# Score tiles of 128 and 256 columns masked and reduced in one VectorE operation, zero products in 32-row tiles, and a new order, in a three-stage attention and experts kernel

## The chip, the cores and the metric

One core of a Trainium2 chip. The metric is the device time of one execution in microseconds; the runs of the kernel before took 534.11, 534.59 and 535.53 us, and their median, 534.59 us, is the time to compare with.

## The reference

Three stages, for 4 batches of 448 positions (S) and 768 channels. Shapes are in the comments.

```python
def _attn_ref(q, k, v, cap):                 # 4 x 12 heads x 448 x 64
    scores = scale * np.matmul(q, k.transpose(0, 1, 3, 2))
    scores = cap * np.tanh(scores / cap)
    attn = softmax(scores)
    return np.matmul(attn, v)

def _moe_ref(x, w_in, conv_w, w_out):        # 768 -> 1024 -> 768
    h = np.maximum(x @ w_in, 0.0)
    conv_out = three taps of conv_w over the positions of h
    gate = 1.0 / (1.0 + np.exp(-conv_out))
    return h * gate @ w_out

def _moe2_ref(x, w_gate, wq, wk, wv, wo):    # 4 experts, head size 64
    two best experts of each position, weights w by softmax over the two
    for e in range(E):
        scores = scale * (q @ k.transpose(0, 2, 1))
        scores = np.where(causal, -1000000000.0, scores)
        a = softmax(scores)
        out += w[e] * (a @ v @ wo[e])        # for positions that chose e
```

The weights w_in, conv_w and w_out come as 64-bit floats; everything else is 32-bit.

## The kernel before

The class Plan records every operation of the kernel once, with its engine, as a numbered entry (`add`). `issue()` then emits them in the order of the table ORDER, a permutation of those numbers written out, so ORDER alone sets the sequence of work on every engine and on the DMA queue. A second table, SWAP, holds numbers of operations whose engine is flipped: `pick` and `one_of` offer an eviction or a copy to ScalarE (ACT) or VectorE (DVE), and a number in SWAP takes the other one. Because helpers record the operations, the profile shows a helper's line for all of them: L376 for products on TensorE (PE), L380 for transposes, L324 for VectorE, L316 for ScalarE, L385 for DMA issues on SyncE (SP), L399 for GpSimd (POOL). The buffers have three names: fm (32-bit floats in SBUF), rm (the rounded halves that the fast products read) and ps (the eight PSUM banks).

The stages overlap. Attention runs in 24 groups of two heads (six groups for each batch): score products, Tanh and Exp on ScalarE over tiles of up to 1792 columns, sums on VectorE, then the products with v. The first two groups' scores are plain 32-bit products (`qk`, `last_keys`); each 32-bit product is two passes of PE.

Beside attention, in the first 58 us, `wi_prep` brings in w_in: 24 pieces of 128 rows by 256 columns. `decode` turns the 64-bit words of a piece into 32-bit floats in four operations (a multiplication by 2^-112 on either engine by `one_of`, a shift, and two SCALAR_TENSOR_TENSOR operations), then `pick` makes the upper half and a subtraction on VectorE the lower half. The pieces use two sets of buffers in turn (`wi_bufs`), in places of the region `later`. When attention of a batch is done, `recip` and `x_unit` (labels x0 to x3) normalise it, and the products with w_in (`f_unit`, labels f0 to f3) follow, three rounded products for each exact one. The gates (`conv_gate`) go over DRAM to the last stage. `fold_mm` multiplies w_out by the experts' weights, and the last stage does the projections, the scores, the transposes and the output for each batch.

The zero products: while the first loads are on their way, PE multiplies a tile z of zeros, which a VectorE memset (L573) fills. z is the first 128 columns of `CT.bufs[0]`, at the start of the region `later`, where `wi_prep` puts its decoded pieces. WARM = 8 products of 128 x 128 by 128 columns carry the label "st", FILL = 4 more "warm"; the order decides where they go.

The experts' scores, `scores2(b, i, k)`: for each batch b and pair of experts i, seven tiles k of 128 rows in a PSUM bank: each of the two experts has one of 128, 256 and 384 columns, and the last 64 positions of both share one of 448. For each tile VectorE adds the triangle of -1e9 (`tri`) to the last 128 columns in PSUM (64 for the shared one), a second VectorE operation takes the negative of the row maximum, and ScalarE does Exp with that as its bias and sums the rows into `accum_out`. There are 56 such tiles, 16 each of 128, 256 and 384 columns and 8 of 448. The lines:

```python
pl.tt(o, o, tri_m if shared else tri, OP.add)
pl.reduce(mx, ps[:, :n], OP.max, negate=True)
pl.act(P2[i][k], ps[:, :n], AF.Exp, bias=mx, accum_out=RS2[i][:, 0, k:k + 1])
```

Of the kernel before, what the change touches and what calls it, by code (L numbers as in the profile page):

```python
# [8 lines left out]
AF = mybir.ActivationFunctionType  # L9
# [10 lines left out]
E = 4  # L20
NK = S // 128
SH = S // 2
# [180 lines left out]
class Plan:  # L203
# [5 lines left out]


    DRAIN = 97.0
    OPEN = {(128, 128): 107.0, (64, 128): 107.0, (128, 64): 53.0, (64, 64): 53.0, (128, 32): 13.0}
    RATE = 320.0
    HOP = {"pe": 200.0, "act": 190.0, "dve": 170.0, "pool": 150.0, "dma": 1500.0}

# [1201 lines left out]
```

## Time and profile before

| what | value |
|---|---|
| median of three runs (lowest, highest) | 534.59 us (534.11, 535.53) |
| profiled execution: span from first to last instruction | 532.9 us |
| what the runs hold beyond that span | 1.2 to 2.6 us, 1.7 us at the median |
| PE busy | 523.3 us (98%), 3312 instructions |
| VectorE busy | 448.8 us (84%), 1053 instructions |
| ScalarE busy | 372.1 us (70%), 689 instructions |
| GpSimd busy | 18.4 us (3%) |
| DMA, mean | 120 GB/s |
| granted clock of TensorE, mean | 1.000 |

The page gives the profiled execution's span and no total of its own, so its own time is taken as its span and the runs' times are set beside it. The span is the time between the first and the last instruction on any engine. Busy times overlap. A share is an average over stages with different limits, so the windows below, which give busy times stretch by stage, say more than the column of shares. A busy PE is not a PE at its peak: ends of products are modelled.

### The profile page before, as it was taken

How to read it: one execution, taken by the hardware profiler on the slowest of the kernel's cores; microseconds unless marked ns; L12 is line 12 of the kernel's file. 1: busy time of each engine (PE TensorE's matmuls, PEld its weight loads, DVE VectorE, ACT ScalarE, POOL GpSimd, SP SyncE). 2: the span in 40 equal slices, each digit the busy share in tenths (PEclk: the TensorE clock that was granted, in tenths of full speed). 3: DMA queues.
4: the chain of work that ended last, by engine and by line, in shares of the span. 5: the costliest groups of instructions: out<-in, count | busy, mean ns of one | idle time of the engine just before them, and what ended most of it. 6: DMA issues, size and time to landing. Idle time of an engine off the chain costs nothing.

```text
span 532.9 us, 9400 instructions
## 1 busy us (share of the span) xinstructions
PE 523.3 (98%) x3312; PEld 414.2 (78%) x3312; DVE 448.8 (84%) x1053; ACT 372.1 (70%) x689; POOL 18.4 (3%) x71
## 2 busy tenths in 40 slices
PE   8989999999999999999999999999999999999997
PEld 6434488545765857669999999999978988999786
DVE  6999999889689787889768999979998997965772
ACT  7989948999888869865333667627858884653562
POOL 8100000000000000000000002000000000000000
PEclk9999999999999999999999999999999999999999
DMA  6535554423323241225574442245345225404414
GB/s 205 177 129 163 173 174 155 115 83 104 117 79 105 66 133 54 79 81 174 185 243 148 127 138 62 87 108 141 78 101 139 91 49 144 125 1 124 124 52 156
DMA packets 42543, 63.84 MB, mean 120 GB/s; under 512 B 7424, under 2 KB 31360, under 8 KB 42496
## 3 DMA queue, kind: packets, MB, share of 16 engines
q1 hardware_dynamic: 42496, 63.24, 39.4%
q8 instruction: 26, 0.43, 0.3%
q14 instruction: 21, 0.17, 0.1%
HBM read 40.94 MB, written 12.85 MB: 101 GB/s over the span
## 4 chain that ended last, share of the span: by engine, by line
PE 80%; DVE 15%; issue 2%; DMA 2%; ACT 1%; SPq 0%; DVEq 0%
PE ps L376 77%; DVE fm L324 10%; DVE rm L324 5%; PE ps L380 3%; DMA fm<-w_in 2%; ACT fm L316 1%; SPq L385 0%; ACT rm L316 0%; DVE ps L324 0%; DVEq L324 0%
## 5 line engine op out<-in xcount | busy, mean ns | idle before, releaser
L376 PE MATMUL ps<-rm 128*128 128x448 f32 (+6 forms) x2316 | 401.4, 351 | 4.4 <-DVE fm L324 1.9
L376 PEld LDWEIGHTS ps<-rm 128*128 128x128 f32 (+1 forms) x2316 | 353.1, 187 | 49.0 <-issue 8.7
L316 ACT ACTIVATE fm<-fm 128x448 f32<-128x448 f32 (+7 forms) x216 | 158.7, 767 | 35.0 <-DVE fm L324 22.7
L324 DVE SCALAR_TENSOR_TENSOR fm<-fm 128x448 f32<-128x448 f32 (+5 forms) x240 | 146.8, 631 | 14.7 <-ACT fm L316 12.7
L316 ACT ACTIVATE fm<-ps,fm 128x896 f32<-128x896 f32 (+5 forms) x142 | 109.7, 793 | 30.7 <-DVE fm L324 20.2
L376 PE MATMUL ps<-fm 128*64 128x448 f32 (+9 forms) x868 | 114.7, 470 | 1.8 <-DVE fm L573 1.1
L376 PEld LDWEIGHTS ps<-fm 128*64 128x64 f32 (+4 forms) x868 | 46.8, 135 | 64.5 <-issue 45.5
L324 DVE TENSOR_TENSOR rm<-fm,rm 128x448 fp32r<-128x448 f32 (+4 forms) x154 | 86.7, 584 | 8.2 <-ACT rm L316 7.3
L316 ACT ACTIVATE fm<-ps 128x448 f32<-128x448 f32 (+4 forms) x124 | 53.3, 451 | 41.3 <-PE ps L376 25.6
L316 ACT ACTIVATE rm<-fm 128x448 fp32r<-128x448 f32 (+5 forms) x94 | 49.4, 547 | 34.3 <-DVE fm L324 16.0
L324 DVE TENSOR_TENSOR fm<-fm 64x448 f32<-64x448 f32 (+6 forms) x112 | 60.8, 550 | 7.0 <-ACT fm L316 5.5
L324 DVE TENSOR_SCALAR fm<-fm 128x256 f32<-128x256 f32 (+11 forms) x144 | 44.4, 324 | 9.3 <-ACT fm L316 4.1
L316 ACT ACTIVATE rm<-ps 128x386 fp32r<-128x386 f32 (+3 forms) x42 | 18.0, 434 | 15.2 <-PE ps L376 14.6
L324 DVE TENSOR_TENSOR ps<-ps,fm 128x128 f32<-128x128 f32 (+1 forms) x56 | 15.6, 285 | 13.6 <-PE ps L376 11.5
L324 DVE COPY fm<-ps 128x448 f32<-128x448 f32 (+4 forms) x39 | 18.9, 492 | 9.0 <-PE ps L376 4.5
L324 DVE TENSOR_REDUCE fm<-ps 128x1 f32<-128x256 f32 (+3 forms) x56 | 24.8, 448 | 0.9
L324 DVE CAST rm<-fm 128x448 fp32r<-128x448 f32 (+4 forms) x68 | 24.2, 368 | 0.9 <-DMA fm<-kq 0.5
L399 POOL MEMSET fm<- 64x3 f32 (+12 forms) x43 | 8.5, 222 | 364.3 <-DVE fm L324 363.3
L324 DVE TENSOR_TENSOR rm<-ps,rm 128x386 fp32r<-128x386 f32 (+1 forms) x32 | 18.7, 586 | 0.9 <-ACT rm L316 0.5
L324 DVE TENSOR_TENSOR fm<-fm,ps 128x448 f32<-128x448 f32 (+1 forms) x30 | 16.7, 570 | 3.0 <-PE ps L376 2.7
L380 PE MATMUL ps<-fm 128*128 128x128 f32 x128 | 17.6, 274 | 0.2 <-ACT fm L316 0.2
L380 PEld LDWEIGHTS ps<-fm 128*128 128x128 f32 x128 | 14.9, 140 | 2.0 <-ACT fm L316 0.4
(22 smaller groups left out, 64.6 us busy)
## 6 DMA issues: line engine op xcount, KB each, us to landing
g_dram<-fm SPq DMA_DIRECT2D x32, 224.0 KB, 2.6
fm<-g_dram SPq DMA_DIRECT2D x32, 224.0 KB, 2.7
fm<-w_in SPq DMA_DIRECT2D x24, 256.0 KB, 2.8
fm<-woT SPq DMA_DIRECT2D x16, 384.0 KB, 3.2
fm<-kq SPq DMA_DIRECT2D x23, 256.0 KB, 3.5
out<-fm SPq DMA_DIRECT2D x23, 224.0 KB, 2.3
fm<-v SPq DMA_DIRECT2D x24, 192.0 KB, 3.2
fm<-kq SPq DMA_DIRECT2D x23, 192.0 KB, 3.0
```

What stands on the lines that cost most here:

```text
L316: return self.add("act", cost, [lambda: self.nc.scalar.activation(out, in_, func, **kw)], [out] + more, [in_] + ptr)
L324: return self.add("dve", cost, [lambda: f(out, *ins, **kw)], [out], aps)
L376: self.nc.tensor.matmul(out, a, b, start=start, stop=stop, **kw))
L380: calls = [lambda o=o, i=i, d=d: self.nc.tensor.transpose(o, i, d) for o, i, d in parts]
L399: self.add("pool", cost, [lambda: f(out, *ins, **kw)], [out], [x for x in list(ins) + [kw.get("in_")] if hasattr(x, "ap")])
```

## The change

Four edits.

1. The experts' score tiles of 128 and 256 columns (32 of the 56) are masked and reduced by one call, `mask_least`: x becomes x times -1 plus the mask, in PSUM, and `least` becomes the row minimum of that. Exp then has scale -1. The tile `masks` is 128 columns of zeros and then `tri`; it lies in a region of the last stage. Since `tri` was also used early as `one_1`, that tile and the gate's small tiles now share its old place.
2. The four FILL products each become 16 products in tiles of 32 rows by 64 columns, 96 columns wide, in four row groups and two column halves, twice over. Each row group writes a bank of its own (0, 7, 1, 2).
3. ORDER is a new permutation.
4. SWAP is a new set.

```diff
 ORDER = tuple(map(int, '''
-0 24 13 26 1 15 23 14 30 2 103 3 1430 38 187 1431 4 41 49 17 5 18 60 86 78 1428 16 79 68 80 39 70 81 128 50 82 83 97
...
 SWAP = frozenset(map(int, '''
-91 95 104 108 111 119 123 133 137 142 146 153 157 160 168 175 179 184 195 206 210 213 228 232 235 239 244 248 262 270
...
+73 91 95 108 111 119 123 133 137 146 153 157 160 168 175 184 185 195 206 213 228 232 235 244 248 259 262 270 274 277
...
+    def mask_least(self, x, mask, least):
+
+        cost = max(68 + self.cols(x) * 1.0417, 190.0)
+        self.add("dve", cost, [lambda: self.nc.vector.tensor_tensor_reduce(x, x, mask, -1.0, 3.0e38, OP.add, OP.min, least)],
+                 [x, least], [x, mask])
...
-    tri, tri_m = fm.take(128), fm.take(KR)
+    gate_at, tri_m = fm.at, fm.take(128 + KR)[:, 128:]
...
-    RC, one_1 = rm.take(SH), tri[:, :96]
+    RC, one_1 = rm.take(SH), fm.take(96, gate_at)
...
         for _ in range(FILL):
-            pl.mm([(bank(7)[:, :128], z, z, True, True)])
+            pl.mm([(bank((0, 7, 1, 2)[n // 32])[a, :96], z[n:n + 32, :64], z[n:n + 32, :96], True, True, {"tile_position": (n, a.start)})
+                   for _ in range(2) for n in range(0, 128, 32) for a in (lo64, hi64)])
...
-    gt, ge = (fm.take(NT * E * E).rearrange("p (k a b) -> p k a b", k=NT, a=E) for _ in range(2))
+    gt, ge = (fm.take(NT * E * E, gate_at + n).rearrange("p (k a b) -> p k a b", k=NT, a=E) for n in (0, 64))
+    masks = fm.take(256)
+    tri = masks[:, 128:]
...
+        fused = n <= 256
         o = ps[:, 128 * (NK if shared else j):n]
-        pl.tt(o, o, tri_m if shared else tri, OP.add)
+        if not fused:
+            pl.tt(o, o, tri_m if shared else tri, OP.add)
...
-        pl.reduce(mx, ps[:, :n], OP.max, negate=True)
-        pl.act(P2[i][k], ps[:, :n], AF.Exp, bias=mx, accum_out=RS2[i][:, 0, k:k + 1])
+        if fused:
+            pl.mask_least(ps[:, :n], masks[:, 256 - n:], mx)
+        else:
+            pl.reduce(mx, ps[:, :n], OP.max, negate=True)
+        pl.act(P2[i][k], ps[:, :n], AF.Exp, bias=mx, scale=-1.0 if fused else 1.0, accum_out=RS2[i][:, 0, k:k + 1])
```

What this does to the sequences is shown at three places. A row is one instruction or a run of equal ones (x n): line, operation, what it writes and reads, columns, and in brackets the semaphores that it waits for (DMAHW is a DMA queue's, PE, DVE and Activation those of the engines).

VectorE at the start of the program, before. The MEMSET fills z, the operations on one column prepare constants from `cap`, and TENSOR_SCALAR and SCALAR_TENSOR_TENSOR of 256 columns are `decode` of w_in's first piece.

```order
L573 MEMSET fm 128x128
L324 RECIPROCAL fm<-fm 128x1 [waits DMAHW0_49]
L324 TENSOR_SCALAR fm<-fm 128x1 [waits DVE_49]
L324 TENSOR_SCALAR fm<-fm 128x1
L324 TENSOR_TENSOR fm<-fm 128x1 [waits DVE_49]
L324 TENSOR_SCALAR fm<-fm 128x1 [waits Activation_49]
L324 TENSOR_SCALAR fm<-fm 128x256 [waits DMAHW3_49]
L324 TENSOR_SCALAR fm<-fm 128x256 [waits DVE_49]
L324 SCALAR_TENSOR_TENSOR fm<-fm 128x256 [waits DVE_49] x2
L324 CAST rm<-fm 128x448 [waits DMAHW5_49]
```

The same place now.

```order
L578 MEMSET fm 128x128
L323 RECIPROCAL fm<-fm 128x1 [waits DMAHW0_49]
L323 TENSOR_SCALAR fm<-fm 128x1 [waits DVE_49]
L323 TENSOR_SCALAR fm<-fm 128x1
L323 TENSOR_TENSOR fm<-fm 128x1 [waits DVE_49]
L323 TENSOR_SCALAR fm<-fm 128x256 [waits DMAHW1_49,PE_49]
L323 TENSOR_SCALAR fm<-fm 128x256 [waits DVE_49]
L323 TENSOR_SCALAR fm<-fm 128x1 [waits Activation_49]
L323 SCALAR_TENSOR_TENSOR fm<-fm 128x256 [waits DVE_49] x2
L323 TENSOR_SCALAR fm<-fm 128x256 [waits Activation_49]
```

The first decode of w_in now waits for PE as well: the buffer set that it writes is the one over z, and the count that it waits for is that of all 72 zero products. Before, the first decode used the other buffer set, and the decode that writes over z stood 21st on VectorE.

TensorE at the start, before. The 128x128 rows on fm are zero products, 128x256, 128x192 and 128x448 the first two groups' scores.

```order
L376 MATMUL ps<-fm 128x128 x5
L376 MATMUL ps<-fm 128x256 x4
L376 MATMUL ps<-fm 128x192 x2
L376 MATMUL ps<-fm 128x448 x2
L376 MATMUL ps<-fm 128x192 x2
L376 MATMUL ps<-fm 128x128 x6
L376 MATMUL ps<-fm 64x448 x4
```

The same place now.

```order
L381 MATMUL ps<-fm 128x128 x8
L381 MATMUL ps<-fm 64x96 x64
L381 MATMUL ps<-fm 128x256 x4
L381 MATMUL ps<-fm 128x448 x2
L381 MATMUL ps<-fm 128x192 x4
L381 MATMUL ps<-fm 64x448 x4
```

All zero products now stand ahead of the first score product; before, five did, six stood between scores and one later. On SyncE the queue before is `first`, two pieces of kq, w_in, v; now it is `first`, two pieces of w_in, then kq's two.

VectorE in the experts' scores of batch 0, before: TENSOR_TENSOR on ps is the mask, TENSOR_REDUCE the maximum.

```order
L324 TENSOR_TENSOR ps<-ps,fm 128x128
L324 TENSOR_REDUCE fm<-ps 128x1
L324 COPY fm<-fm 128x3
L324 RECIPROCAL fm<-fm 128x7
L324 COPY fm<-fm 64x1
L324 TENSOR_TENSOR fm<-fm 128x7
```

The same stage now.

```order
L350 ISA ps,fm<-ps,fm 128x128
L350 ISA fm 128x1
L323 TENSOR_TENSOR rm<-fm,rm 128x448
L323 TENSOR_TENSOR ps<-ps,fm 128x128
L323 TENSOR_TENSOR rm<-ps,rm 128x448
L323 TENSOR_REDUCE fm<-ps 128x1
```

The call of `mask_least` is two instructions on the queue (both L350): one over the tile and one of a single column. Tiles of 384 and 448 columns keep their pair. Over the whole program PE has 2938 products instead of 2878, which is 64 tile products for 4 full ones; all others are the same. VectorE has 28 more CAST and COPY and 17 more TENSOR_SCALAR and SCALAR_TENSOR_TENSOR, ScalarE 45 fewer operations; nearly all of these moves lie in the batches after the first.

## Rows read from the trace of the kernel before

**Rows 1.** The page of the profile: span, and the last chain by engine.

```profile
span 532.9 us, 9400 instructions
...
PE 80%; DVE 15%; issue 2%; DMA 2%; ACT 1%; SPq 0%; DVEq 0%
```

**Rows 2.** Windows; from:to length, busy PE, PEld, DVE, ACT, POOL, granted clock, DMA share, GB/s.

```profile
4.00:8.00 4.00, 4.00 (x26) 2.58 (x25) 2.31 (x7) 2.94 (x5) 3.77 (x22) 1.00 0.92 297
8.00:58.80 50.80, 46.88 (x357) 22.78 (x355) 50.08 (x117) 49.01 (x55) 6.35 (x23) 1.00 0.53 170
58.80:135.00 76.20, 75.49 (x488) 49.16 (x488) 71.04 (x150) 63.70 (x84) 0.00 (x0) 1.00 0.41 130
135.00:380.00 245.00, 244.84 (x1505) 205.18 (x1505) 206.73 (x417) 161.54 (x279) 3.49 (x12) 1.00 0.38 116
380.00:520.00 140.00, 139.46 (x875) 123.84 (x873) 114.11 (x356) 90.35 (x261) 1.71 (x2) 1.00 0.35 95
520.00:532.90 12.90, 9.78 (x61) 7.99 (x58) 3.87 (x7) 3.17 (x8) 0.00 (x0) 1.00 0.44 161
```

**Rows 3.** The chain that ended last; start us, us, what.

```profile
2.18 3.54 DMA fm<-w_in
...
58.83 33.25 PE ps L376 x190
...
135.16 245.56 PE ps L376 x1504
```

**Rows 4.** Timeline of DVE, 5 to 17 us; start, us, operations [idle before].

```profile
5.74 0.82 DVE L324 TENSOR_SCALAR fm<-fm 128x256 f32<-128x256 f32 x2 [1.46 <-DMA fm<-w_in]
6.59 1.05 DVE L324 SCALAR_TENSOR_TENSOR fm<-fm 128x256 int32<-128x256 int32 x2
...
8.57 0.41 DVE L324 TENSOR_TENSOR rm<-fm,rm 128x256 fp32r<-128x256 f32 x1
8.90 0.39 DVE L324 CAST rm<-fm 128x448 fp32r<-128x448 f32 x1
```

**Rows 5.** Timeline of ACT, 3 to 10 us.

```profile
4.82 0.69 ACT L316 ACTIVATE fm<-ps,fm 128x512 f32<-128x512 f32 x1 [0.72 <-PE ps L376]
5.67 1.26 ACT L316 ACTIVATE fm<-ps,fm 128x512 f32<-128x512 f32 x2 [0.17 <-PE ps L376]
```

**Rows 6.** Weight loads by form; windows 1.1:3.1, 5.5:5.9, 5.9:7.1, 7.3:8.7; count | busy, mean ns.

```profile
L376 PEld LDWEIGHTS ps<-fm 128*128 128x128 f32 x10 | 2.2, 329 | 1.1 <-DVE fm L573 1.1
...
L376 PEld LDWEIGHTS ps<-fm 64*128 64x128 f32 x4 | 0.4, 280 | 0.7 <-ACT fm L316 0.7
...
L376 PEld LDWEIGHTS ps<-fm 64*128 64x128 f32 x10 | 1.0, 205 | 0.4 <-ACT fm L316 0.2 <-issue 0.2
...
L376 PEld LDWEIGHTS ps<-fm 128*128 128x128 f32 x12 | 1.4, 191 | 0.2 <-issue 0.2
```

**Rows 7.** Products by form, whole span.

```profile
L376 PE MATMUL ps<-fm 64*64 64x448 f32 x192 | 21.3, 551 | 0.0
```

**Rows 8.** VectorE by form, whole span.

```profile
L324 DVE SCALAR_TENSOR_TENSOR fm<-fm 128x256 int32<-128x256 int32 x48 | 20.1, 425 | 0.8
...
L324 DVE COPY fm<-ps 128x448 f32<-128x448 f32 x24 | 14.7, 617 | 5.6 <-PE ps L376 3.7 <-PE ps L380 1.7
...
L324 DVE TENSOR_TENSOR ps<-ps,fm 128x128 f32<-128x128 f32 x48 | 13.8, 294 | 10.2 <-PE ps L376 8.1 <-ACT rm L316 0.8 <-ACT fm L316 0.7
...
L324 DVE TENSOR_REDUCE fm<-ps 128x1 f32<-128x256 f32 x16 | 6.7, 422 | 0.3
...
L324 DVE TENSOR_REDUCE fm<-ps 128x1 f32<-128x128 f32 x16 | 4.6, 285 | 0.2
...
L324 DVE CAST rm<-fm 128x256 fp32r<-128x256 f32 x14 | 4.2, 302 | 0.1
...
L324 DVE TENSOR_SCALAR fm<-fm 128x1 f32<-128x1 f32 x3 | 0.4, 150 | 0.3 <-ACT fm L316 0.3
```

**Rows 9.** ScalarE by form, whole span.

```profile
L316 ACT ACTIVATION_READ_ACCUMULATOR fm<-ps,fm 128x1 f32 x56 | 10.9, 195 | 0.0
```

More of the change, by code (lines that the diff above doesn't have):

```diff
@@ L211 @@
     DRAIN = 97.0
-    OPEN = {(128, 128): 107.0, (64, 128): 107.0, (128, 64): 53.0, (64, 64): 53.0, (128, 32): 13.0}
+    OPEN = {(128, 128): 107.0, (64, 128): 107.0, (128, 64): 53.0, (64, 64): 53.0, (128, 32): 13.0, (32, 64): 53.0}
     RATE = 320.0
@@ L1062, in chain_kernel @@
                     base=0, channel_multiplier=-1)
+    pl.pool("memset", masks[:, :128], 0.0)
     pl.pool("memset", bef, 1.0)
```

216 rows, old and new, of tables (ORDER, SWAP) are left out of this document.

## The prediction

> **What bounds the kernel now.** I read the page first, then the windows by stage, then the chain of waits, then the start in the timelines.
>
> The page gives a span of 532.9 us and a last chain that is 80% PE and 15% VectorE [rows 1]. The shares hide where each holds, and the windows show it [rows 2]. From 8 to 58.8 us VectorE is busy 50.08 of 50.80 us and ScalarE 49.01, while PE idles 50.80 - 46.88 = 3.92 us: there VectorE is the bound, with ScalarE 1 us behind it. From 58.8 us on PE is the bound: it idles 0.71 us to 135, 0.16 to 380 and 0.54 to 520. The last 12.9 us hold the end of the products and the last stores. VectorE's room there is wide: 245 - 206.73 = 38.3 us from 135 to 380 and 140 - 114.11 = 25.9 us from 380 to 520. The chain agrees: it begins with the load of w_in, goes over VectorE, and from 58.83 and 135.16 us runs in long stretches of products [rows 3].
>
> So an edit can move the end in two ways: by when VectorE's work of the first 58.8 us is done, or through the 1.4 us that PE idles between 58.8 and 520. The span is 1.7 us short of the median of the runs; I make the sum against the span and add 1.7.
>
> **Products.** All products but the zero ones are the same, and the zero ones run before PE is the bound. No term of its own.
>
> **The start: zero products ahead of w_in.** VectorE began w_in's first decode at 5.74 us, after 1.46 us of waiting for the load [rows 4]. In the changed kernel that decode waits in addition for all 72 zero products, and everything of VectorE's bound stretch is queued behind it. So when are they done? The first five products made ten weight loads in 2.2 us, so 0.22 us a pass, from 1.1 us on [rows 6]. Later twelve of the same loads took 1.4 us, 0.117 each, though the granted clock reads 1.00 (its upper level) in every window [rows 2, 6]. Passes of the 64-row form average 205 ns from 5.9 us on and 280 ns between 5.5 and 5.9, so in this execution the rate rose at about 5.7 us [rows 6]. PE had been busy without a break since 1.1 us, as it will be again, so I keep 5.7.
>
> Eight full products are 16 passes: 16 x 0.22 = 3.5, so they end at 4.6 us. The 64 tile products are 128 passes of 96 columns. No tile of 32 rows is in the trace; the nearest row is that of 64x64 tiles, four of which fill the array: a pass averages 551 ns, yet 192 records take 21.3 us, 0.111 each, so all four run side by side, 0.444 us for 448 columns [rows 7]. At that pace 96 columns take 0.095 us, and at the slow rate 0.095 x 0.22/0.117 = 0.178. I take it that eight tiles, which fill the array too, run side by side: 16 rounds. From 4.6 to 5.7 us there is time for 6.2 slow ones, and the other 9.8 take 0.93 us: the end is 6.6 us. With 0.17 us for the wait, as ScalarE showed after PE [rows 5], VectorE starts at 6.8 us: **+1.05 us**. The bounds: with all tiles at the full rate the end is 4.6 + 1.5, hence +0.55; with four tiles at a time there are 32 rounds, 25.8 of them fast, and the start is at about 8.3 us, +2.6; with four at a time and the slow rate throughout, 32 x 0.178 = 5.7, so 10.45 us and +4.7.
>
> The Trainium skill, page TensorEngine Tiling (Array Packing), section Key Properties, says that different tiles can load weights and multiply in parallel. The row above shows it for four tiles alone; by that rule the start would be 6.8 us, and by no more than the four that the row shows, 8.3 us.
>
> ScalarE's first Tanh, at 4.82 us, waits for the first score products [rows 5]. Those now follow the zero products: eight passes at some 0.1 us each [rows 6] from 6.6 us on, so about 7.5 us, 2.7 later. ScalarE idles 1.06 us from 4 to 8 and 1.79 us to 58.8 [rows 2], 2.85 in all, which just covers that; without this cover it costs what exceeds it. The two pieces of kq go out two places later. One of them takes w_in's former place, whose load went from 2.18 to 5.72 us [rows 3]; even one place after, it is there by 6.6.
>
> **VectorE's load up to 58.83 us.** Along its queue up to what the products at 58.83 us need, 128 instructions stand for 127: two more COPY out of PSUM (617 ns) and two more CAST of 256 columns (302), two fewer SCALAR_TENSOR_TENSOR (425) and one fewer multiplication of 256 columns, priced like the CAST [rows 8]: 1.23 + 0.60 - 0.85 - 0.30 = **+0.7 us**. Against that, 13 instructions instead of 18 read what the one just ahead wrote. Neighbours that don't depend overlap (one starts at 8.57, takes 0.41, and the next starts at 8.90) and dependent ones leave a gap (5.74 and 0.82, next at 6.59) [rows 4]: some 0.1 us apiece, **-0.5 us**. VectorE's idle time of 0.72 us [rows 2] can absorb half of itself: **-0.35 us**. So the products at 58.83 us start some 0.9 us later.
>
> **The joined operation.** A tile of 128 columns cost VectorE 294 + 285 ns and one of 256 columns 294 + 422 [rows 8]. Now it is one operation over the tile, which I price like the reduction alone (285, 422; the mask is read along), and a second of one column. That read-out is not in VectorE's trace. Below it costs nothing, as I know no reason why it could not hide; above, 195 ns, ScalarE's read-out of its accumulator [rows 9]. I take 150, the row of one column on VectorE [rows 8]. The saving is 294 - 150 = 0.14 us a tile, 32 x 0.14 = 4.6 us, in stages where VectorE has room, so it shows only through PE's idle time of 0.54 us in 380 to 520 [rows 2] and a little before: **-0.5 us**. If the operation runs at half its rate instead, it costs 0.285 and 0.422 more, 0.14 and 0.28 net, 16 x (0.14 + 0.28) = 6.8 us more on VectorE.
>
> **Moves from ScalarE to VectorE.** Some 45 operations, at most 617 ns each [rows 8]: 28 us at most, nearly all after 135 us, where 64 us of VectorE's time are free. Nothing, as long as none stands in front of an operation that PE waits for. What bound them before is that order, and it is new; a mishap there is bounded by the rivals.
>
> **Sum.** 1.05 + 0.7 - 0.5 - 0.35 - 0.5 = +0.4: span 533.3, **535.0 us** against the median of 534.59.
>
> **Rivals.**
>
> *Slower: the start costs more.* Four tiles run at a time, or the rate rises later. In favour: no row shows eight at once, and nothing fixes the 5.7 us. Against: in both tile forms' neighbours the whole array was in use. Four at a time adds 1.5 us to the sum, 536.5 us; with the slow rate throughout, 3.6 us, 538.6. It decides once w_in's first decode starts after about 8 us. ScalarE then starts 4.2 us late, which its 2.85 us of idle time no longer cover.
>
> *Faster: the order removes PE's idle time.* Between 8 and 520 us PE idles 3.92 + 1.41 = 5.3 us [rows 2]. If half of that goes, the start's delay included, the span is 530.2 and the time 531.9 us; if nearly all, 529.5. In favour: fewer dependent neighbours on VectorE, two ScalarE evictions fewer early on, w_in loaded earlier, and the joined operation near the end of the chain. Against: the greatest part of that idle time lies in VectorE's stretch, whose load grows and starts later.
>
> *The joined operation is no gain.* On the queue it is two instructions, so "one operation" is not what is done. At half rate VectorE's 6.8 us more meet PE only where VectorE is nearly full around 380 us; I put 1.5 us on the path: 536.5 us. The Trainium skill, page Vector Engine (DVE) Microarchitecture Reference, section Points that are easy to get wrong, says that a two-source form with both sources in SBUF and not in bf16 runs at half throughput. Here one source lies in PSUM, and no run here shows the form.
>
> **Numbers.** A measurement of this kernel can tell about 0.3% (1.6 us) from no change, so "same" is 533.0 to 536.2 us. The forecast has 0.40 and lies there. The order has 0.32, all of it faster. The late start has 0.24 and the half rate 0.04, both slower. The likeliest case's own range is 533.2 to 536.2. With the order's case down to 531.0 (its far part left out) and the start's up to 538.2, some 2 in 10 are outside.
>
> **What would show it.** In the changed kernel's timeline: w_in's first decode at 6.8 us (8.3 or later is the slower rival; before 5.8 my first term is wrong), ScalarE's first Tanh at about 7.5, the long stretch of products that began at 58.83 at about 59.7. VectorE's forms: joined operations of about 285 and 422 ns and 150 for the read-out. Windows: PE's idle time from 8 to 58.8 us still near 4 us and under 1 us from 135 to 520. If PE idles less than 2 us before 58.8 while its busy time is the same, the order has won and the forecast is wrong.

## The result and the profile after

The changed kernel took 538.65 us (median of four, 537.53 to 538.96) against 534.35 us for the kernel before (median of four too): 1.0073 times as long, 95% interval 1.0061 to 1.0086. I had forecast 535.0 with a range up to 538.2 and gave "slower" 0.28; the time lies 0.45 us above the range. The profiled execution is the fastest of the four, 537.53 us with a span of 535.8, so it shows 2.9 us of the 4.3. The other three spans were 536.8 to 537.2 us, and no trace holds what they add.

The page of the changed kernel, span, TensorE and the last chain by engine:

```profile
span 535.8 us, 9604 instructions
...
PE 525.3 (98%) x3432; PEld 415.9 (78%) x3432; DVE 458.4 (86%) x1098; ACT 361.0 (67%) x644; POOL 16.1 (3%) x72
...
PE 57%; DVE 24%; DMA 8%; ACT 5%; issue 4%; SPq 1%; DVEq 0%; ACTq 0%
```

The chain was 80% PE before and is 57% now [rows 1]. The windows of the changed kernel, with the columns of [rows 2]:

```profile
4.00:8.00 4.00, 4.00 (x141) 3.59 (x141) 0.79 (x3) 0.70 (x3) 3.67 (x18) 1.00 0.94 304
8.00:58.80 50.80, 46.42 (x346) 22.27 (x342) 48.89 (x117) 48.12 (x51) 5.23 (x24) 0.97 0.53 165
58.80:135.00 76.20, 75.72 (x499) 49.17 (x496) 71.30 (x150) 65.08 (x85) 0.00 (x0) 1.00 0.43 132
135.00:380.00 245.00, 244.34 (x1505) 204.34 (x1503) 216.86 (x441) 154.69 (x255) 3.86 (x12) 1.00 0.39 116
380.00:520.00 140.00, 139.49 (x866) 123.11 (x864) 115.82 (x379) 85.80 (x242) 0.22 (x2) 1.00 0.34 91
520.00:535.80 15.80, 12.41 (x80) 10.54 (x78) 4.01 (x8) 5.33 (x13) 0.00 (x0) 0.99 0.40 146
```

PE's idle time hardly grew. Window by window from 8 us on it is 4.38 us (3.92 before), 0.48 (0.71), 0.66 (0.16), 0.51 (0.54) and 3.39 us (3.12), +1.0 us in all. The other 1.9 us are PE's busy time, 525.3 us on the page for 523.3. The forms of zero products and plain scores that differ, whole span, of the kernel before:

```profile
L376 PE MATMUL ps<-fm 128*128 128x128 f32 x24 | 4.6, 351 | 1.1 <-DVE fm L573 1.1
...
L376 PE MATMUL ps<-fm 64*128 64x256 f32 x8 | 2.1, 671 | 0.0
...
L376 PE MATMUL ps<-fm 64*128 64x192 f32 x8 | 1.2, 385 | 0.0
```

and of the changed one:

```profile
L381 PE MATMUL ps<-fm 128*128 128x128 f32 x16 | 3.8, 431 | 1.1 <-DVE fm L578 1.1
...
L381 PE MATMUL ps<-fm 32*64 32x96 f32 x128 | 2.4, 316 | 0.0
...
L381 PE MATMUL ps<-fm 64*128 64x256 f32 x8 | 1.1, 402 | 0.0
L381 PE MATMUL ps<-fm 64*128 64x192 f32 x8 | 0.9, 349 | 0.2 <-ACT fm L315 0.2
```

The zero products take 3.8 + 2.4 us where they took 4.6, +1.6 us; the first plain scores, which now run later and at the higher pace, take 1.1 + 0.9 instead of 2.1 + 1.2, -1.3 us. That leaves 1.6 of the 1.9 us, and the clock of TensorE can account for it. Two windows of two us of the kernel before:

```profile
10.00:12.00 2.00, 1.86 (x16) 1.04 (x14) 2.00 (x3) 2.00 (x3) 2.00 (x4) 1.00 0.58 168
12.00:14.00 2.00, 1.76 (x13) 0.99 (x12) 1.97 (x5) 2.00 (x4) 1.91 (x10) 1.00 0.69 215
```

and five of the changed kernel:

```profile
8.00:10.00 2.00, 1.82 (x16) 0.96 (x12) 1.93 (x6) 2.00 (x3) 1.64 (x12) 1.00 0.22 80
10.00:12.00 2.00, 1.16 (x12) 0.21 (x8) 1.97 (x6) 2.00 (x5) 1.77 (x6) 1.00 0.75 232
12.00:14.00 2.00, 0.99 (x4) 0.69 (x6) 1.97 (x5) 2.00 (x3) 1.79 (x8) 0.79 0.67 198
14.00:16.00 2.00, 2.00 (x14) 1.78 (x12) 1.97 (x8) 0.83 (x2) 0.02 (x1) 0.50 0.75 229
16.00:18.00 2.00, 1.71 (x12) 0.83 (x10) 2.00 (x7) 1.95 (x3) 0.00 (x0) 0.86 0.83 231
```

PE was busy only 1.16 and 0.99 of 2 us from 10 to 14. Within the second of these windows the granted clock, 1.00 throughout before, falls to 0.50, the lower of its two levels, and stays there until about 16.6 us: (0.21 + 0.50 + 0.14) x 2 = 1.7 us of full-rate time gone. PE idled for a part of it, so 1.7 us is the most that its busy time can have grown by this. 1.6 - 1.3 + 1.7 = 2.0, against 1.9 measured.

Where VectorE loses time in its stretch shows on its timeline in the changed kernel, at the first decode of w_in and at its only long wait behind that:

```profile
7.30 0.95 DVE L323 TENSOR_SCALAR fm<-fm 128x256 f32<-128x256 f32 x3 [3.18 <-PE ps L381]
...
33.06 0.29 DVE L323 TENSOR_SCALAR fm<-fm 128x256 f32<-128x256 f32 x1 [1.33 <-DMA fm<-w_in]
```

The decode starts at 7.30 us, behind PE; before, at 5.74 [rows 4]. At 33.06 VectorE has waited another 1.33 us for a piece of w_in. SyncE's timeline in the changed kernel shows when that load went out:

```profile
23.94 0.36 SPq L390 DMA_DIRECT2D fm<-v  x1
27.31 0.80 SPq L390 DMA_DIRECT2D fm<-kq  x2
28.23 1.45 SPq L390 DMA_DIRECT2D fm<-w_in  x2
```

It was issued at 28.23 us (the chain has it land 4.74 us later). SyncE had stood from 24.30 to 27.31 ahead of two loads of kq, and SyncE's waits from 20 to 30 us (in all, times, longest) put those 3 us to PE:

```profile
SPq L390 <- PE ps L381: 3.0, 1, 3.0
```

The load is not later than in the kernel before. By the two ORDER tables it is entry 167, there the second of this pair on SyncE:

```profile
29.46 3.01 SPq L385 DMA_DIRECT2D fm<-w_in  x2
```

so it went out at about 32.1 us, 3.9 us later than in the changed kernel. But there VectorE began to decode that piece only here, with no wait:

```profile
36.85 0.61 DVE L324 TENSOR_SCALAR fm<-fm 128x256 f32<-128x256 f32 x2
```

In the changed order VectorE asks for it at 33.06 - 1.33 = 31.73 us, 5.1 us earlier. So the wait is made by two queues that were moved by different amounts. The 3.0 us for PE and the slow landing (4.74 us, where the page's median for w_in is 2.9) both hold the load. By these figures it would have been in time without the one or without the other (3.0 and 1.84 us are more than 1.33), but no run takes either away. VectorE's longest wait from 8 to 58.8 us in the kernel before was 0.26 us, at 20.95:

```profile
20.95 0.29 DVE L324 TENSOR_SCALAR fm<-fm 128x256 f32<-128x256 f32 x1 [0.26 <-DMA fm<-w_in]
```

PE's next stretch shows the sum. Its timeline at the first plain products of 128x64 tiles by 448 columns, in the kernel before:

```profile
59.24 5.27 PE L376 MATMUL ps<-fm 128*64 128x448 f32 x28
```

and in the changed one:

```profile
61.94 4.36 PE L381 MATMUL ps<-fm 128*64 128x448 f32 x22
```

They are 2.70 us late. VectorE started 1.56 us later and idled 50.80 - 48.89 = 1.91 us in the window from 8 us instead of 0.72, 1.19 more: together 2.75 us. So in this execution nearly all of the loss stands at 62 us, and the rest of the span changes it by 0.2. That small rest hides a second loss. The kernel before with the joined operation alone (old_order_joined, below) has a span of 531.1 us, and there the same products are at

```profile
58.58 6.39 PE L381 MATMUL ps<-fm 128*64 128x448 f32 x40
```

From these products to the end it takes 472.5 us, the kernel before 473.7 and the changed one 473.9. The joined operation should have brought some 1.1 us there, and what goes with the new order takes it away again. In the six profiled executions that have the old order up to there, these products start between 58.58 and 59.66 us, so differences at this place are known to about half a us.

The joined operation by form (the trace names it as a custom operation) and its read-out, in the changed kernel:

```profile
L350 DVE CUSTOM_DVE_ANT_0 ps<-ps,fm 128x256 f32<-128x256 f32 x16 | 6.9, 429 | 3.8 <-PE ps L381 3.7
...
L350 DVE CUSTOM_DVE_ANT_0 ps<-ps,fm 128x128 f32<-128x128 f32 x16 | 4.7, 296 | 3.3 <-PE ps L381 2.6 <-ACT fm L315 0.5
...
L350 DVE DVE_READ_ACCUMULATOR2_ANT fm<- 128x1 f32 x32 | 4.4, 138 | 0.0
```

### The profile page after: what moved, and what is told of

It is laid out like the page before. It is cut to its first block, busy times and chain, and to the rows that moved or that the text cites. A ratio compares the mean times of both kernels' runs of the same rounds, so it can differ in the third digit from the quotient of the medians.

```text
span 535.8 us, 9604 instructions
## 1 busy us (share of the span) xinstructions
PE 525.3 (98%) x3432; PEld 415.9 (78%) x3432; DVE 458.4 (86%) x1098; ACT 361.0 (67%) x644; POOL 16.1 (3%) x72
## 4 chain that ended last, share of the span: by engine, by line
PE 57%; DVE 24%; DMA 8%; ACT 5%; issue 4%; SPq 1%; DVEq 0%; ACTq 0%
PE ps L381 56%; DVE fm L323 16%; DVE rm L323 8%; ACT fm L315 5%; DMA g_dram<-fm 2%; DMA fm<-w_in 2%; PE ps L385 2%; DMA fm<-woT 2%; SPq L390 1%; DMA fm<-v 1%; DMA rm<-rm 0%; ACT rm L315 0%; DVE ps L323 0%; DVE ps L350 0%; DVE fm L350 0%
## 5 line engine op out<-in xcount | busy, mean ns | idle before, releaser
L323 DVE SCALAR_TENSOR_TENSOR fm<-fm 128x448 f32<-128x448 f32 (+4 forms) x240 | 148.0, 633 | 9.7 <-ACT fm L315 6.8
L381 PE MATMUL ps<-fm 128*64 128x448 f32 (+7 forms) x988 | 115.3, 450 | 2.1 <-DVE fm L578 1.1
L381 PEld LDWEIGHTS ps<-fm 128*64 128x64 f32 (+5 forms) x988 | 47.4, 140 | 64.4 <-issue 45.8
L315 ACT ACTIVATE fm<-ps 128x448 f32<-128x448 f32 (+5 forms) x102 | 44.0, 455 | 43.4 <-PE ps L381 23.9
L315 ACT ACTIVATE rm<-fm 128x448 fp32r<-128x448 f32 (+4 forms) x86 | 45.2, 547 | 25.8 <-DVE fm L323 18.5
L323 DVE TENSOR_SCALAR fm<-fm 128x256 f32<-128x256 f32 (+10 forms) x148 | 46.3, 321 | 13.5 <-ACT fm L315 4.8
L323 DVE COPY fm<-ps 128x448 f32<-128x448 f32 (+5 forms) x52 | 23.4, 462 | 8.5 <-PE ps L381 6.3
L323 DVE CAST rm<-fm 128x448 fp32r<-128x448 f32 (+5 forms) x76 | 27.5, 367 | 2.0 <-DMA fm<-kq 0.8
L350 DVE CUSTOM_DVE_ANT_0 ps<-ps,fm 128x128 f32<-128x128 f32 (+1 forms) x32 | 11.4, 363 | 7.1 <-PE ps L381 6.3
L323 DVE TENSOR_REDUCE fm<-ps 128x1 f32<-128x384 f32 (+1 forms) x24 | 13.7, 573 | 0.3
```

The lines of the kernel that those rows point to most:

```text
L315: return self.add("act", cost, [lambda: self.nc.scalar.activation(out, in_, func, **kw)], [out] + more, [in_] + ptr)
L323: return self.add("dve", cost, [lambda: f(out, *ins, **kw)], [out], aps)
L350: self.add("dve", cost, [lambda: self.nc.vector.tensor_tensor_reduce(x, x, mask, -1.0, 3.0e38, OP.add, OP.min, least)], [x, least], [x, mask])
L381: self.nc.tensor.matmul(out, a, b, start=start, stop=stop, **kw))
```

## Experiments

All are kernels of this program; "the order" is the table ORDER, "the engines" the table SWAP. Both tables go by operation numbers, and these were carried over between the two versions where a mask and a maximum became one. The pieces of code below are shortened, and tables are described in words.

| run | median us (lowest to highest) | ratio to before, 95% interval |
|---|---|---|
| old_order_joined | 533.31 (532.56 to 534.39) | 0.9979 [0.9970, 0.9989] |
| new_order_old_ops | 543.48 (541.40 to 545.08) | 1.0167 [1.0137, 1.0197] |
| zeros_apart | 537.60 (535.40 to 540.52) | 1.0068 [1.0045, 1.0091] |
| zeros_apart_filled | 537.07 (536.17 to 538.04) | 1.0054 [1.0033, 1.0075] |
| scores_after_eight | 537.41 (536.14 to 539.14) | 1.0058 [1.0043, 1.0074] |
| scores_after_five | 538.78 (537.47 to 539.18) | 1.0077 [1.0064, 1.0090] |
| start_by_first_loads | 540.08 (538.45 to 541.02) | 1.0096 [1.0078, 1.0113] |
| start_split_first | 538.64 (536.76 to 540.43) | 1.0081 [1.0060, 1.0102] |
| new_order_old_engines | 577.93 (577.53 to 578.38) | 1.0813 [1.0799, 1.0827] |
| scores_after_five_old_engines | 575.27 (573.99 to 576.85) | 1.0766 [1.0748, 1.0784] |
| fold_old_engines | 537.75 (537.60 to 538.54) | 1.0063 [1.0050, 1.0077] |
| new_to_24_then_old | 534.69 (534.06 to 537.29) | 1.0010 [0.9997, 1.0023] |
| new_to_135_then_old | 538.21 (537.79 to 538.98) | 1.0070 [1.0057, 1.0084] |
| old_to_12_then_new | 540.99 (539.61 to 541.29) | 1.0117 [1.0104, 1.0130] |
| old_to_24_then_new | 540.41 (540.04 to 541.68) | 1.0115 [1.0098, 1.0132] |
| old_to_135_then_new | 536.29 (536.19 to 537.08) | 1.0037 [1.0022, 1.0052] |
| old_to_280_then_new | 535.25 (534.77 to 535.95) | 1.0017 [1.0007, 1.0026] |
| old_to_400_then_new | 534.10 (533.62 to 534.55) | 0.9992 [0.9983, 1.0001] |

**The operations and the order, each alone.** The first keeps the order of before and takes the joined operation:

```diff
-ORDER, SWAP of the changed kernel
+ORDER, SWAP of the kernel before, mask_least at the place of the mask
-16 tile products per FILL
+pl.mm([(bank(7)[:, :128], z, z, True, True)])
```

> The kernel before, its order, engines and full zero products kept, with the joined operation alone (each pair of mask and maximum of the 32 small tiles becomes the joined operation at the place of the mask). Theory A (the loss is made in the first 20 us, by the new order and the zero products): the joined operation costs nothing on the path, 533.5 to 534.5 us, 0 to -0.5 us against the kernel before; VectorE busy 4 to 5 us less. Theory B (the joined operation or its read-out costs on the path of the last stage): 536 us or more.

The second is the kernel before with the changed tables:

```diff
-ORDER, SWAP of the kernel before
+ORDER, SWAP of the changed kernel, mask and maximum at the place of mask_least
```

> The changed order and engines with the old operations: mask and maximum apart, four full zero products in place of the 64 tile products, at the same place ahead of the scores. Theory A: still 537 to 538.5 us; w_in's first decode on VectorE still waits for the zero products, which now end at about 6.3 us instead of 7.2, so up to 0.9 us less than the changed kernel; the granted clock still dips to 0.5 near 13 us. Theory B: 535 us or less. Theory C (the tile products themselves are what costs): under 536.5 us.

The joined operation alone gains 1.0 us (533.31 against 534.34 for the kernel before beside it): theory B falls, and this is the version that beats both kernels. The changed order with the old operations is 9.1 us slower than before, worse than theory A allowed, although the zero products are the plain ones and w_in's first decode starts earlier, at 6.28 us; theory C falls as well. So the loss comes with the two tables, order and engines together, and not with the operations. The changed order lives off the shorter operation: without it PE idles 140 - 136.89 = 3.1 us in the window from 380 to 520, with it 0.5. The window with the old operations:

```profile
380.00:520.00 140.00, 136.89 (x834) 119.44 (x835) 118.84 (x368) 82.64 (x234) 0.22 (x2) 1.00 0.34 90
```

**The start.** Six versions of the changed kernel, in which things of its start are undone one after the other. First the wait for the zero products:

```diff
-        z = CT.bufs[0][:, :128]
+        z = OT.bufs[0][:, :128]
```

> The changed kernel with one edit: the zero tile lies in a buffer that is written only after 16 us (OT's first instead of CT's first), so w_in's first decode waits for its load alone. Theory A1 (that wait is the loss): the decode starts at 5.7 us or earlier instead of 7.30, the VectorE-bound stretch ends 1.5 us or more earlier, 536.0 to 537.0 us. Theory A2 (the loss is the granted clock that fell to 0.5 from 12.9 to 16.6 us after PE had idled): the decode starts earlier all the same, the dip stays, and the time moves by less than 0.7 us: 538 us or more.

Then eight zero products more in PE's gaps:

```diff
         for _ in range(FILL):
             pl.mm([...tile products...])
+        for _ in range(8):
+            pl.mm([(bank(7)[:, :128], z, z, True, True)])
```

> As zeros_apart, with eight full zero products more, two ahead of the shared keys' scores and six ahead of the first rounded scores, where PE idled between 9 and 13.5 us. Theory A2: PE no longer idles there, the granted clock stays at 1.00, and the time falls by 1.5 to 2 us against zeros_apart. Theory A1: the eight products take 1.8 us of PE where it is not the bound, so no change within 0.4 us against zeros_apart, or a little slower, whatever the clock does.

VectorE did start earlier, 3.2 us earlier than in the changed kernel. Its timeline in zeros_apart, and its later wait:

```profile
4.14 0.78 DVE L323 TENSOR_SCALAR fm<-fm 128x256 f32<-128x256 f32 x3
...
14.41 0.54 DVE L323 TENSOR_SCALAR fm<-fm 128x256 f32<-128x256 f32 x2 [0.80 <-DMA fm<-w_in]
...
32.31 0.29 DVE L323 TENSOR_SCALAR fm<-fm 128x256 f32<-128x256 f32 x1 [1.81 <-DMA fm<-w_in]
```

But of what was gained at 4.14 little is left: VectorE waits 0.80 us at 14.41 and 1.81 at 32.31 for w_in, where the changed kernel had 1.33, and the products that stood at 61.94 us in the changed kernel stand at 61.31. The time is 1.05 us lower at the median, and the eight executions spread over 5 us, so neither A1's nor A2's figure is met. The clock shows in that spread: the four executions with a mean granted clock of 0.997 to 1.000 took 535.40 to 537.28 us, the four with 0.993 and 0.994 took 537.91 to 540.52. The profiled execution is one at 1.000, although PE was busy even less there than in the changed kernel, 1.92 of 4 us:

```profile
12.00:14.00 2.00, 1.48 (x16) 1.05 (x12) 1.57 (x4) 2.00 (x2) 1.84 (x8) 1.00 0.84 201
14.00:16.00 2.00, 0.44 (x6) 0.17 (x2) 1.55 (x6) 2.00 (x3) 0.65 (x3) 1.00 0.99 354
```

So here more idle time came without a fall. The filled version's profile shows 1.00 throughout, yet its 0.5 us against zeros_apart is within the spread, far from 1.5 to 2. Nor did the filling keep the clock up every time: its two executions at 1.000 took 536.17 and 536.36 us, the two at 0.997 took 537.79 and 538.04. Against the changed kernel the two edits together bring 1.6 us of the 4.3.

Next, the scores ahead of the tile products, which go away; eight or five full zero products stay in front and the others stand in the gaps:

```diff
-8 full, 64 tile products, scores
+8 (5) full, scores, 2 (5) full, shared keys' scores, 6 full, rounded scores
```

> The changed kernel with the zero tile apart, no tile products, eight full zero products ahead of the first scores and eight more in the gaps (two ahead of the shared keys' scores, six ahead of the first rounded ones). Against zeros_apart_filled it differs only in that the 64 tile products don't stand ahead of the first scores. Theory S (ScalarE's late first Tanh is the loss of the start): the first Tanh comes at about 5.5 us instead of 7.9 and the time falls by 1.5 to 2.5 us against zeros_apart_filled's 537.07, to 534.6 to 535.6. Theory D (VectorE's w_in decode alone sets the stretch to 58.8 us): no change within 0.4 us, since that decode starts at about 4.1 us in both.

> As scores_after_eight, but only five zero products ahead of the first scores, as in the kernel before, and five ahead of the shared keys' scores. Theory S: the first Tanh at about 4.8 us, as before, and another 0.4 to 0.8 us less than scores_after_eight, about 534.5. Theory D: no change against it.

The first Tanh came at 6.67 and 6.46 us instead of 7.94, held by a load of w_in for ScalarE's multiplication ahead of it, and the time did not fall: 537.41 and 538.78 us after 537.07. Theory S is refuted as far as that goes, so I moved those too:

```diff
-SP: first, w_in, w_in, kq, kq      ACT: w_in's multiplication, Tanh, Tanh
+SP: first, kq, kq, w_in, w_in      ACT: Tanh, Tanh, w_in's multiplication
```

> scores_after_five with two moves more: kq's two pieces are loaded ahead of w_in's first two, as in the kernel before, and ScalarE's multiplication of w_in's second piece stands behind the first two Tanh instead of ahead of them. Theory L (the loads' order and that multiplication are what hold the start, the zero products were only hiding it): first Tanh at about 4.8 us, no granted clock under 1.00, 2 to 3 us less than scores_after_five's 538.78: 535.5 to 536.8. If it stays over 538, the start is held by something else or made up for later anyway.

The first Tanh stands at 4.82 us, exactly as before, and the kernel takes 540.08 us, more than the changed one. Theory L is refuted. PE's first rounded products in the kernel before, by PE's timeline:

```profile
9.76 1.89 PE L376 MATMUL ps<-rm 64*128 64x448 f32 x12
```

in the changed kernel:

```profile
12.02 0.47 PE L381 MATMUL ps<-rm 64*128 64x448 f32 x2 [0.38 <-DVE rm L323]
13.48 2.98 PE L381 MATMUL ps<-rm 64*128 64x448 f32 x14 [0.99 <-DVE rm L323]
```

and in start_by_first_loads:

```profile
11.99 0.47 PE L381 MATMUL ps<-rm 64*128 64x448 f32 x2
13.45 1.89 PE L381 MATMUL ps<-rm 64*128 64x448 f32 x16 [0.99 <-DVE rm L323]
```

Between these two they hardly move. The split that they need stands behind two pieces of w_in on VectorE, so the last of the series put it, and its loads, behind one:

```diff
-DVE: decode of two pieces of w_in, split of the second group
+DVE: decode of one piece, split of the second group, decode of the next
```

> start_by_first_loads with one move more: the split of the second group's q and k (two casts and two subtractions on VectorE, and their loads ahead of w_in's second piece) stands behind w_in's first piece instead of behind the second. Theory V (that split holds PE's first rounded products at 12 and 13.5 us): they start at 9.8 to 10.5 us, the granted clock stays at 1.00 before 20 us, and the time falls by 2 us or more against 540.08. Rival: the products start early, but w_in's second piece is late in turn and the stretch to 58.8 us ends as before: within 0.7 us of 540.08.

The products still started at 13.51 us. The time is 1.4 us lower than start_by_first_loads with overlapping spreads, and theory V is refuted. No single wait of the start, taken away, brings the time back. All six versions, this one too, keep VectorE's wait for w_in near 33 us: 1.81, 0.55, 1.74, 1.45, 1.04 and 1.47 us in them. It is absent where the old order runs from 24 us on (new_to_24_then_old, below).

**Engines.** The changed kernel, and scores_after_five, with the old table SWAP:

```diff
-SWAP of the changed kernel
+SWAP of the kernel before
```

> The changed kernel with the table SWAP of the kernel before: the new order stays, the choice of ScalarE or VectorE for each eviction and cast is as before. Theory M (the moves to VectorE make it the bound between 290 and 314 us and near 360): the start is unchanged, PE no longer loses 1 us there, 537.3 to 537.9 against the changed kernel's 538.65. Theory N (the moves are free, as predicted): within 0.4 us of 538.65, or slower, because ScalarE's evictions then come later than the new order has room for.

> Both: scores_after_five with the table SWAP of before. Theories S and M together: 533.3 to 534.0 us, as the old order with the joined operation (533.31). If it stays over 535, the new order loses elsewhere.

They are 39.3 and 36.5 us slower than the same kernels with the new SWAP, at mean granted clocks of 0.980 to 0.992. An order is written for one choice of engines, and the other choice puts both queues in a sequence that nobody arranged. Theory M is refuted in this form. Theory N allowed for "slower", so this result does not test it.

**Grafts.** Here the operations that one order issues up to some time come first, then the rest in the sequence of the other. Each operation keeps the engine of the order it comes from; the joined operation and full zero products stand in all of them. So 533.31 us (all old) is the reference.

```diff
-ORDER
+ORDER_a up to its product at T, then what is left in the sequence of ORDER_b
```

> The order and engines of the kernel before up to the products that it starts at 24 us, the changed order and engines for all that is left; joined operation throughout, full zero products. Theory H (the loss is made by the order of the first 24 us, that is by the loads, w_in's decode and the scores' start; the rest of the new order is about even): 533.0 to 535.0 us, PE's work no later than in the kernel before at 24 us. Theory T (the rest of the new order loses as well, as the 1.5 us between 290 and 400 suggest): 535 to 537. Theory J (new order and its start belong together; the piece at the seam costs more than either): over 537.

> The reverse: the changed order and engines up to the products that start at 24 us in the changed kernel, the order before for the rest; joined operation, four full zero products in place of the tile products. Theory H: all of the loss is there, 533.3 + 3 to 4 us, 536.0 to 537.5. If it is under 534.5, the start is not the cause.

> As the first, the order before up to 135 us. The changed kernel made up 1.5 to 2 us against the kernel before between 25 and 135 us, so if that recovery is a gain of the new order and no mere catching up, this is 1 us or more slower than old_to_24_then_new; if it was catching up of the late start, the two are equal within 0.7 us.

> The order before up to 280 us. Of the new order only the stretch from the experts' weights to the end is left, in which the changed kernel lost about 1 us against the kernel before (and 1.9 us against the old order with the joined operation). Theory T: 534.3 to 535.3, against 533.31 for the old order throughout. Theory H: within 0.7 us of 533.31.

> Old order and engines up to the products that the kernel before starts at 400 us, then new; joined operation throughout. The traces put 1.4 of the 1.9 us of old_to_280_then_new between 285 and 390 us and 0.5 after 450: 533.5 to 534.2. If it is 535 or more, the stretch after 400 is the one that loses.

> New order and engines up to the products that the changed kernel starts at 135 us, then old; joined operation, four full zero products in place of the tile products. By the traces the changed kernel is 2.4 us behind the old order with the joined operation at 135 us: 535.5 to 536.5. If it is 534.7 as new_to_24_then_old, the stretch from 24 to 135 us costs nothing of its own.

> The old order and engines up to the products that the kernel before starts at 12 us, then the new; joined operation, full zero products. Theory V: PE no later than the kernel before at 16 us, and 535 to 537 us in all (what the new order loses after 280 us stays). If the seam costs as much as that at 24 us did, over 539.

Theory H falls: the new start followed by the old order costs 1.4 us, not 3 to 4, and the old order after the new start has no wait for w_in. (Its zero products are the full ones, with which the decode starts some 1 us earlier than in the changed kernel.) Against 533.31 the versions with the new order from 400, 280 and 135 us to the end cost 0.8, 1.9 and 3.0 us, and the one with it up to 135 costs 4.9. Two expectations were missed outright: old_to_135_then_new is 4.1 us faster than old_to_24_then_new where slower or equal was expected, and new_to_135_then_old is 1.7 us above its range.

These figures don't add up to 5.3, the changed kernel's distance from 533.31, since a seam costs of itself: both versions joined at 12 and 24 us are slower than the changed kernel. A part of that is the clock. In old_to_24_then_new PE was busy 7.95 of the 12 us from 24 on and the granted clock there averages 0.72. No run gives a seam's cost apart, so each figure is the most that the new order can cost in its stretch. The 0.8 from 400 us is within the two spreads. What stands is that the new order is faster in no stretch that I cut out, and that from 135 us on, where the clock is no part of it, the cost grows with the length of new order that is taken in.

The clock divides the runs of this document in two. In the five versions that keep the old order to 135 us or longer all 38 executions have a mean granted clock of 0.999 or 1.000. Every version with the new order at the start, or a seam at 12 or 24 us, has executions at 0.997 or less, the changed kernel all four. Where one version has both kinds, which holds for eight of them, its executions at 0.999 or more are faster by 0.5 to 2.6 us on the average of either kind in seven, and 0.1 us slower in the eighth, scores_after_five. So the clock can be worth up to some 2 us of the 4.3, but it may go together with other waits of the same executions, and no run separates them.

One of the places can be seen. VectorE is nearly full from 300 to 340 us in either order. Windows of the kernel before:

```profile
285.00:300.00 15.00, 15.00 (x87) 15.00 (x86) 14.73 (x32) 7.49 (x15) 0.00 (x0) 1.00 0.37 105
300.00:320.00 20.00, 20.00 (x115) 20.00 (x114) 19.58 (x40) 12.83 (x27) 0.00 (x0) 1.00 0.41 134
320.00:340.00 20.00, 20.00 (x140) 20.00 (x139) 19.33 (x42) 13.81 (x31) 3.49 (x12) 1.00 0.19 54
```

and of old_to_280_then_new:

```profile
285.00:300.00 15.00, 14.96 (x85) 14.63 (x84) 14.01 (x30) 6.37 (x13) 0.00 (x0) 1.00 0.38 116
300.00:320.00 20.00, 19.45 (x110) 19.13 (x110) 19.65 (x41) 13.40 (x26) 0.00 (x0) 1.00 0.39 114
320.00:340.00 20.00, 20.00 (x136) 20.00 (x135) 19.42 (x41) 12.38 (x27) 3.12 (x10) 1.00 0.17 48
```

From 285 to 300 us the old order has VectorE at work 0.7 us longer, and PE never idles; in the new one PE idles 0.6 us between 285 and 320. Whether operations moved to VectorE do that:

> old_to_280_then_new with 13 operations of the stage that multiplies w_out by the experts' weights (its decodes, splits and gates after 280 us) back on the engines of the kernel before; one operation net leaves VectorE. Theory M (moves to VectorE make PE idle 0.6 us at 300 to 320): no idle time there, 534.2 to 534.8 against 535.25. Theory O (the order of that stage does): the same 535.25 within 0.4, or slower.

Its edit gives 13 operations of that stage back to their old engines. It is 2.5 us slower than old_to_280_then_new, and PE idles 2.3 us from 285 to 320 instead of 0.6. So theory M is refuted: in the new order the new choice of engines gains here. Theory O, which allowed for "slower", stands, and it is again order and engines together.

## Why the prediction was wrong

The step that failed is the term for VectorE's stretch, with its cushion of -0.35 us: I had VectorE idle 0.35 us less up to 58.8 us, and it idled 1.19 us more. Beside it two stretches that I put at nothing were not free: the products, where the clock fell, and the new order of the later stages, which takes back what the joined operation gains there (1.3 us against 1.1). How the 4.3 us divide among these stays open.

- **Zero products ahead of w_in.** The mechanism was right, the size low. The 128 records took 2.4 us, 0.019 each; four tiles at a time would need 0.095/4 = 0.024 even at the full pace, so more than four ran side by side, as eight would. But weight loads of the tiles still averaged 203 ns from 5.5 to 6 us and 155 from 6 to 7, so the pace rose later than the 5.7 us that I kept. The decode started at 7.30 us instead of 6.8: +1.56 us for +1.05. The trace bears out the Trainium skill's page TensorEngine Tiling (Array Packing), section Key Properties, for these tiles too. Of the slower rival, four at a time did not occur, nor its sign (a decode after 8 us); the later rise of the rate, which it named as well, did. Its 538.6 us, close to the measured 538.65, is luck: it came from a decode at 10.45 us.
- **ScalarE's cover.** The first Tanh came at 7.94 (7.5 predicted), 3.1 us late against 2.85 us of cover. Starting it earlier gained nothing.
- **VectorE's load, and half of its idle time as a cushion (-0.35 us).** This step failed. I counted the instructions and not the loads that they wait for: of SyncE's new queue I followed the first five places. The new order has VectorE reach one piece of w_in 5.1 us earlier than the kernel before decodes it, and its load goes out only 3.9 us earlier, behind a load of kq that waits 3.0 us for PE, and lands 4.74 us later. VectorE waits 1.33 us for it, and in all it idles 1.19 us more than before where I had it idle 0.35 less. That is most of what was missing at 62 us (2.70 for 0.9). Putting w_in's load ahead of kq's on SyncE was not tried. Nor is w_in done within the first 58 us, as I wrote of the kernel before: its last load goes out after 91 us there and at 95.5 in the changed kernel.
- **Products: "no term of its own".** Failed: PE idled 1.85 of the 4 us from 10 to 14, and within them the clock fell to 0.50, up to 1.7 us of full-rate time, in a stretch that was free of it before. It doesn't appear as idle time. How much of it reaches the end isn't settled by the filled version.
- **The joined operation.** Right in kind and near in size: 296 and 429 ns for 285 and 422, 138 for a read-out priced at 150. Alone it gains 1.0 us for the 0.5 taken. The half-rate rival is refuted. What the Trainium skill says on the page Vector Engine (DVE) Microarchitecture Reference, section Points that are easy to get wrong, is said of one layout of instructions with two sources (S2S2D2_STT), and of both sources in SBUF. No run here shows the joined operation with both sources there, since one lies in PSUM.
- **Moves from ScalarE to VectorE: "64 us of free time".** Failed as reasoning. The window from 135 to 380 us is too wide: from 300 to 340 VectorE is busy 38.9 of 40 us in the kernel before. The runs do not show that the moves themselves cost, and fold_old_engines shows 13 changed engines of one stage gaining; engines and order can't be judged apart.
- **The rival that the order removes PE's idle time** had 0.32. PE idles 10.5 us for 9.6, and no graft shows the new order faster anywhere. How much slower it is in each stretch is known only up to a seam's cost.

## What to carry to other kernels

When an order is changed, follow each queue, the DMA queue first, to the end of the stretch that bounds the kernel: set the time at which an engine will ask for a load against the time at which the queue lets that load go. Read free time in windows as short as the stage that the moved work belongs to. Price an edit alone in the old order too: here one part gains 1.0 us, and the kernel with the new order and engines around it stands 5.3 us above that.

## What the runs showed of the hardware

TensorE's granted clock, 1.00 in every window shown of the kernel before, fell to 0.50 for some 3.4 us in the changed kernel, within 4 us (10 to 14) of which PE was busy 2.15. The profiled execution of zeros_apart had PE busy 1.92 of the 4 us from 12 to 16 and kept 1.00. The mean differs between executions of one kernel: 0.993 to 1.000 over eight of zeros_apart, with the times given above. The tiles of 32 rows and 64 columns took 0.019 us a record of 96 columns on zeros, less than four at a time would need at the pace of the 64x64 tiles. One VectorE operation that masks and reduces 128 or 256 columns in PSUM takes nearly the time of the reduction alone (296 for 285 ns, 429 for 422), with 138 ns for its read-out behind it.
